# Columns of normalised x for two of four token chunks: DVE 32x32 block transposes and transfers within SBUF in the place of PE transpositions

## The chip, the cores and the metric

The kernel runs on one core of one Trainium2 chip. The metric is the device time of one execution in microseconds (us). Five engines work side by side, each with an instruction queue of its own that runs in order: PE (matmul), DVE (vector), ACT (scalar), POOL (GpSimd) and SP, whose queue here does little but issue DMA transfers.

## The reference

x is 2048 tokens of 576 numbers. Everything is float32.

```python
xn = _layernorm(x, axis=-1)                      # (x - mean) / sqrt(var + eps), per token
s  = _A_ref(xn, A_wqkv, A_wo)                    # attention, 32 heads of 18, then times wo
g  = _silu(_B_ref(xn, B_w_gate, B_w_up, B_w_down))   # ((xn Wg) * (xn Wu)) Wd, F = 4608
return x + s * g
```

Both branches multiply by xn from the left. PE sums over the partitions of its operands, so xn is wanted with its 576 columns on the partitions and the tokens along the free axis. This turning is what the change touches.

## The kernel before

**Precision.** Each float32 operand is split into a rounded high part and a low part (the rest); a product takes three terms. `xc`, the turned xn of a chunk, holds high parts in slots 0 to 3 (512 columns), low parts in slots 4 to 7, and the last 64 columns twice in slot 8 (high in partitions 0 to 63, low in 64 to 127).

**Stages.** A prologue of some 190 us makes q, k and v from xn; a main loop of some 2300 us does attention and the gated branch, two streams that share PE, in an order that a planner in the kernel has worked out and written down; a short end multiplies by wo. The change lies in the prologue, and the instructions from the main loop on stay as they are.

**The prologue** takes the tokens in four chunks of 512 (c = 0 to 3; a chunk is four tiles t of 128 tokens). Its order is the order of the code: each engine gets its instructions as the lines come.

- `load_x(c)` fetches a chunk to `xin` (two buffers). `norm(c)` makes its statistics and writes `xn` (one buffer), half a chunk at a time: chunk c+2 is normalised between blocks of chunk c.
- `to_columns(c)` turns `xn`: for each of five groups of 128 columns, four PE transpositions (128x128, with the identity) to a PSUM bank, an ACT copy for the high part, a DVE subtraction for the low part. So that the fifth group too has 128 columns, the last 64 columns are copied a second time into `xn[:, t, 576:640]` (line 374). `first_columns()` does the same for chunk 0.
- `qk_block(b, c)` makes 128 rows of q or k for a chunk: 14 matmuls to one PSUM bank (tags a and b in turn, two buffers each, so four in all), ACT copies the high part to `hl`, DVE subtracts for the low part, and SP stores `hl` to DRAM (`sqk`). `hl` has three buffers. I write c1b0 for block 0 of chunk 1.
- `v_block(t)` makes a tile of v with two banks of the four of tag g; ACT copies them to `vo` (three buffers before line 604), SP stores them (`sv`).
- `x_store(c, ks)` writes `xc` to DRAM for the gated branch, `w_fetch` and `v_fetch` load weights, `w_now` and `v_split` split them (ACT and POOL).

For c = 1 the order is: `load_x(3)`, c1b0 to c1b2, `to_columns(2)`, c1b3, `v_split(1)`, half of `norm(3)`, part of `x_store`, c1b4, the other half of `norm(3)`, part of `x_store`, c1b5, rest of `x_store`, `w_fetch(3)`, `v_block(0)` to `v_block(3)`, `w_fetch(4)`. For c = 2: c2b0 to c2b2, `to_columns(3)`, c2b3 to c2b5 with `x_store` of chunk 2. Then c3b0 follows.

**SP's queue** issues all these transfers in that order. The program gives them eight semaphores in turn, so each waits until the transfer eight places ahead of it has landed, besides what it waits for otherwise.

Of the kernel before, what the change touches and what calls it, by code (L numbers as in the profile page):

```python
# [41 lines left out]
def kernel(  # L42
# [10 lines left out]
    nc = tc.nc  # L53
    _, S, D = x.shape
# [5 lines left out]
    NCH = S // 512  # L60
# [8 lines left out]
    wpool = ctx.enter_context(tc.tile_pool(name="wpool", bufs=1))  # L69
    xcp = ctx.enter_context(tc.tile_pool(name="xcp", bufs=2))  # L70
# [25 lines left out]
    x2 = x.rearrange("o s d -> (o s) d")  # L96
# [3 lines left out]
    ep = early.enter_context(tc.tile_pool(name="early", bufs=1, side="right"))  # L100
# [123 lines left out]
    graw, gw, draw, dw = {}, {}, {}, {}  # L224
# [100 lines left out]
    xcs = [None] * NCH  # L325
    vstack, pro = ExitStack(), ExitStack()
    vp = vstack.enter_context(tc.tile_pool(name="vp", bufs=1))
    pp = pro.enter_context(tc.tile_pool(name="pro", bufs=1))
# [15 lines left out]
    xin, xns = {}, {}  # L344

    def load_x(c):
        xin[c] = ep.tile([128, 4, D], FT, name="xin", bufs=2)
        for t in range(4):
            nc.sync.dma_start(xin[c][:, t, :], x2[c * 512 + t * 128:c * 512 + t * 128 + 128, :])

# [2 lines left out]
    def norm_stats(c, t):  # L353
        st = ep.tile([128, 2, 6], FT, name="st", bufs=4)
        mv = ep.tile([128, 2], FT, name="mv", bufs=4)
        rs = ep.tile([128, 2], FT, name="rs", bufs=4)
        for g in range(2):
            nc.vector.bn_stats(st[:, g, :], xin[c][:, t, g * HALF:(g + 1) * HALF])  # L358
        nc.vector.bn_aggr(mv, st)
        nc.scalar.activation(rs[:, 0:1], mv[:, 1:2], AF.Sqrt, bias=eps)  # L360
        stat[c, t] = mv, rs

    def norm_apply(c, t):
        if t == 0:
            xns[c] = ep.tile([128, 4, 640], FT, name="xn", bufs=1)
        xn = xns[c]
        mv, rs = stat.pop((c, t))
        nc.vector.reciprocal(rs[:, 1:2], rs[:, 0:1])
        op = nc.vector.tensor_scalar(xn[:, t, 0:D], xin[c][:, t, :], mv[:, 0:1], rs[:, 1:2],  # L369
                                     op0=OP.subtract, op1=OP.mult)  # L370
        if c < 2 and t == 3:
            behind.append(op)
        if c:
            nc.vector.tensor_copy(xn[:, t, D:640], xn[:, t, 512:D])
        else:
            nc.scalar.activation(xn[:, t, D:640], xn[:, t, 512:D], AF.Copy)

    def norm(c, ts=range(4)):
        for t in ts:
            norm_stats(c, t)  # L380
        for t in ts:
            norm_apply(c, t)

    nqk = [0]

    def to_columns(c):

        xn = xns.pop(c)
        if c < 2:
            xc = pp.tile([128, 9, 512], FR, name="xcx", bufs=2)  # L390
        else:
            xc = xcp.tile([128, 9, 512], FR, name="xc")
        xcs[c] = xc
        for k in range(5):
            if k < 4:
                p = bank("g", 3)
            else:
                p = bank("a" if nqk[0] % 2 else "b", 2)
                nqk[0] += 1
            for t in range(4):  # L400
                nc.tensor.transpose(p[:, t * 128:(t + 1) * 128],
                                    xn[:, t, k * 128:(k + 1) * 128], ident)
            if k < 4:
                nc.scalar.activation(xc[:, k, :], p, AF.Copy)
                nc.vector.tensor_tensor(xc[:, 4 + k, :], p, xc[:, k, :].bitcast(FT),
                                        op=OP.subtract)
            else:
                nc.scalar.activation(xc[:, 8, :], p, AF.Copy)
                nc.vector.tensor_tensor(xc[64:128, 8, :], p[64:128, :],
                                        xc[64:128, 8, :].bitcast(FT), op=OP.subtract)  # L410
# [47 lines left out]
    def qk_block(b, c):  # L458
        w, ninth = (t[:, b % 2] for t in wq[b // 2])
        p = bank("a" if nqk[0] % 2 else "b", 2)  # L460
        nqk[0] += 1
        for n, (a, e) in enumerate(QK_PAIRS):
            nc.tensor.matmul(p, w[:, a, :] if a < 9 else ninth, xcs[c][:, e, :], start=n == 0,  # L463
                             stop=n == len(QK_PAIRS) - 1)
        hl = pp.tile([128, 2, 512], FR, name="hl", bufs=3)
        nc.scalar.activation(hl[:, 0, :], p, AF.Copy)
        nc.vector.tensor_tensor(hl[:, 1, :], p, hl[:, 0, :].bitcast(FT), op=OP.subtract)
        g0 = blocks[b]
        for kind in range(2):
            lo, hi = max(g0, kind * D), min(g0 + 128, (kind + 1) * D)  # L470
            if lo < hi:
                dst = sqk[kind, :, lo - kind * D:hi - kind * D, c * 512:(c + 1) * 512]
                nc.sync.dma_start(dst.rearrange("h r s -> r h s"), hl[lo - g0:hi - g0].bitcast(FT))
# [21 lines left out]
    def v_fetch(h):  # L495
        raw = vp.tile([128, 5, HALF], FT, name="wvraw", bufs=1)
        vbox["raw"] = raw
        c0 = 2 * D + h * HALF
        nc.sync.dma_start(raw[:, 0:4, :],
                          wqkv[0:512, c0:c0 + HALF].rearrange("(k p) c -> p k c", p=128))  # L500
        for b in (0, 64):
            nc.sync.dma_start(raw[b:b + 64, 4, :], wqkv[512:576, c0:c0 + HALF])
# [12 lines left out]
    def v_block(t):  # L515
        c, r = divmod(t, 4)
        ps = [bank("g", 3), bank("g", 3)]
        for h in range(2):
            for n, (a, e) in enumerate(PAIRS):
                nc.tensor.matmul(ps[h][:, 0:HALF], xcs[c][:, e, r * 128:(r + 1) * 128],  # L520
                                 vbox["w"][:, a, h * HALF:(h + 1) * HALF], start=n == 0,
                                 stop=n == len(PAIRS) - 1)
        v = vrows[vturn[0] % len(vrows)]
        vturn[0] += 1
        for h in range(2):
            nc.scalar.activation(v[:, 16 * h:16 * h + 16, 0:DH],
                                 ps[h][:, 0:HALF].rearrange("p (a b) -> p a b", b=DH), AF.Copy)
        nc.sync.dma_start(sv[t * 128:(t + 1) * 128], v)

    def w_now(i):  # L530
        wq[i], todo = w_split(raws[i], 1 if i == 4 else 2, ep if i == 2 else pp if i == 4 else None)
        for f, a in todo:
            f(*a)

    def w_fetch(i):
        raws[i] = w_load([(wqkv, b) for b in blocks[2 * i:2 * i + 2]])
# [30 lines left out]
    for c in range(NCH):  # L567
        if c + 2 < NCH:
            load_x(c + 2)
        for b in range(3):  # L570
            qk_block(b, c)
            if c == 0 and b == 0:
                w_now(2)
        if c + 1 < NCH:
            to_columns(c + 1)
        for b in range(3, 6):
            qk_block(b, c)
            if c == 1 and b == 3:
                v_split(c)
            if b < 5 and c + 2 < NCH:  # L580
                norm(c + 2, (0, 1) if b == 3 else (2, 3))
            if c in (1, 2):
                x_store(c, range(3 * (b - 3), 3 * (b - 2)))
            if c == 0 and b == 3:
                v_split(c)
            if c == 0 and b == 5:
                v_fetch(1)
            if c == NCH - 1 and b == 3:
                w_now(3)
        if c == 1:  # L590
            w_fetch(3)
            for t in range(4):
                v_block(t)
            w_fetch(4)
        if c == 2:
            w_now(4)
# [780 lines left out]
    with ExitStack() as end:  # L1377
        ep = end.enter_context(tc.tile_pool(name="end", bufs=1, reuse_waits="tile"))
# [44 lines left out]
        for i, t in enumerate(order):  # L1423
# [13 lines left out]
            y = ys[i % 4]  # L1437
# [3 lines left out]
            xt = xi.pop(t)  # L1441
# [40 lines left out]
```

## Time and profile before

| | |
|---|---|
| median of 3 runs | 2594.03 us (2592.9 to 2594.87) |
| profiled execution | 2593.44 us, span of its instructions 2591.3 us |
| busy: PE, DVE, ACT, POOL | 2582.0, 1813.5, 1550.6, 675.8 us |
| DMA | 435.65 MB in 186066 packets, mean 168 GB/s |
| granted PE clock | 1.0 |

The span counts from the first instruction; 2.1 us of the execution lie around it. In a row of the timeline stand the start, the length, engine, line, operation, output and inputs, the count of instructions merged into the row, and in brackets the idle time before the first of them and what ended it. A row of a line's instructions gives the shortest, median and longest duration in ns. For SP a duration is that of the issue, not of the transfer. A row of windows gives, for a stretch, busy time of each engine and at its end the granted PE clock, the mean busy share of the 16 DMA engines and the rate in GB/s.

### The profile page before, as it was taken

How to read it: one execution, taken by the hardware profiler on the slowest of the kernel's cores; microseconds unless marked ns; L12 is line 12 of the kernel's file. 1: busy time of each engine (PE TensorE's matmuls, PEld its weight loads, DVE VectorE, ACT ScalarE, POOL GpSimd, SP SyncE). 2: the span in 40 equal slices, each digit the busy share in tenths (PEclk: the TensorE clock that was granted, in tenths of full speed). 3: DMA queues.
4: the chain of work that ended last, by engine and by line, in shares of the span. 5: the costliest groups of instructions: out<-in, count | busy, mean ns of one | idle time of the engine just before them, and what ended most of it. 6: DMA issues, size and time to landing. Idle time of an engine off the chain costs nothing.

```text
span 2591.3 us, 59623 instructions
## 1 busy us (share of the span) xinstructions
PE 2582.0 (100%) x24440; PEld 2132.3 (82%) x24440; DVE 1813.5 (70%) x2996; ACT 1550.6 (60%) x3096; POOL 675.8 (26%) x697
## 2 busy tenths in 40 slices
PE   9999999999999999999999999999999999999999
PEld 7899877888888888888878887777887877877889
DVE  7209777777777778777777877777777777777238
ACT  4223677766766666666666666666666666666621
POOL 3114444434431222222111222111111222221016
PEclk9999999999999999999999999999999999999999
DMA  7899767677653444454444443444444444443357
GB/s 243 251 299 260 202 184 194 184 193 212 175 190 114 142 163 135 151 161 160 142 168 149 142 140 127 138 145 159 121 158 124 145 150 141 133 140 112 124 204 252
DMA packets 186066, 435.65 MB, mean 168 GB/s; under 512 B 51041, under 2 KB 111105, under 8 KB 155585
## 3 DMA queue, kind: packets, MB, share of 16 engines
q1 hardware_dynamic: 183632, 423.88, 53.0%
q0 software_dynamic: 2160, 7.96, 0.8%
q8 instruction: 192, 3.15, 0.5%
q14 instruction: 82, 0.66, 0.1%
HBM read 315.16 MB, written 111.35 MB: 165 GB/s over the span
## 4 chain that ended last, share of the span: by engine, by line
PE 97%; DVE 1%; DMA 1%; ACT 0%; issue 0%; SPq 0%; ACTq 0%; DVEq 0%
PE pg L775 36%; PE pg L734 17%; PE pg L836 16%; PE pa L671 11%; PE pb L723 9%; PE pg L520 2%; PE pb L463 2%; PE pa L463 1%; PE pg L1431 1%; DMA sqk<-hl 1%; PE pb L1431 1%; PE pa L1431 1%; DVE st L358 0%; DMA wgu<-swg 0%; DVE xn L369 0%; PE pa L723 0%
## 5 line engine op out<-in xcount | busy, mean ns | idle before, releaser
L673 DVE TENSOR_REDUCE mx<-pa 128x1 f32<-128x512 f32 x2016 | 1348.8, 687 | 331.9 <-PE pa L671 156.3
L775 PE MATMUL pg<-xc,wgu 64*128 64x512 f32 x7776 | 1442.5, 392 | 0.4 <-DMA wgu<-swg 0.3
L725 ACT ACTIVATE pt<-pb 128x512 f32<-128x512 f32 x2005 | 1144.5, 602 | 471.3 <-PE pb L723 369.0
L775 PEld LDWEIGHTS pg<-xc,wgu 64*128 64x128 f32 x7776 | 1078.8, 186 | 45.5 <-issue 0.8
L836 PE MATMUL pg<-wd,hs 64*128 64x288 f32 x6816 | 877.7, 293 | 0.0
L836 PEld LDWEIGHTS pg<-wd,hs 64*128 64x128 f32 x6816 | 815.2, 185 | 11.6 <-issue 0.8
L671 PE MATMUL pa<-whole,turning 54*128 54x512 f32 x1999 | 783.2, 399 | 0.3 <-DVE mx L673 0.3
L723 PE MATMUL pb<-whole,turning 56*128 56x512 f32 x1978 | 775.2, 398 | 0.0
L734 PE MATMUL pg<-pt,vt 128*32 128x512 f32 x4096 | 453.3, 594 | 0.1
L671 PEld LDWEIGHTS pa<-whole,turning 54*128 54x128 f32 x1999 | 363.3, 184 | 75.3 <-issue 53.0
L816 POOL TENSOR_TENSOR hs<-us,hs 128x512 fp32r<-128x512 f32 x144 | 186.0, 1292 | 866.4 <-ACT hs L800 610.0
L863 POOL TENSOR_TENSOR acc<-acc,st 128x288 f32<-128x288 f32 x284 | 229.5, 810 | 606.0 <-ACT st L893 341.0
L723 PEld LDWEIGHTS pb<-whole,turning 56*128 56x128 f32 x1978 | 360.0, 184 | 5.7 <-ACT pt L725 0.2
L734 PEld LDWEIGHTS pg<-pt,vt 128*32 128x32 f32 x4096 | 126.2, 110 | 285.1 <-issue 279.2
L740 DVE TENSOR_TENSOR oc<-oc,pg 128x512 f32<-128x512 f32 x35 | 24.1, 688 | 221.2 <-PE pg L734 214.9
L257 POOL TENSOR_TENSOR wgu<-wraw,wgu 128x384 fp32r<-128x384 f32 x108 | 108.1, 1014 | 215.3 <-ACT wgu L256 97.6
L738 ACT ACTIVATE oc<-pg 128x512 f32<-128x512 f32 x32 | 19.1, 598 | 229.4 <-PE pg L734 222.0
L899 DVE TENSOR_TENSOR acc<-acc,pg 128x288 f32<-128x288 f32 x261 | 116.3, 448 | 38.5 <-PE pg L836 34.5
L792 DVE TENSOR_TENSOR us<-pg,us 128x512 f32<-128x512 f32 x144 | 98.6, 685 | 54.0 <-PE pg L775 50.9
L893 ACT ACTIVATE st<-pg 128x288 f32<-128x288 f32 x284 | 117.1, 413 | 27.0 <-PE pg L836 19.9
L785 ACT ACTIVATE us<-pg 128x512 f32<-128x512 f32 x143 | 85.5, 598 | 76.6 <-PE pg L775 65.4
L800 ACT ACTIVATE hs<-us 128x512 fp32r<-128x512 f32 x142 | 89.4, 630 | 15.9 <-DVE us L792 15.4
(154 smaller groups left out, 1288.8 us busy)
## 6 DMA issues: line engine op xcount, KB each, us to landing
wgu<-swg SPq DMA_DIRECT2D x102, 1152.0 KB
wd<-swd SPq DMA_DIRECT2D x50, 1152.0 KB
swg<-wgu SPq DMA_DIRECT2D x36, 1152.0 KB
whole<-sqk SPq DMA_DIRECT2D x192, 144.0 KB
turning<-sqk SPq DMA_DIRECT2D x384, 72.0 KB
swd<-wd SPq DMA_DIRECT2D x18, 1152.0 KB
sqk<-hl SPq DMA_DIRECT2D x32, 512.0 KB
xc<-sx SPq DMA_DIRECT2D x24, 512.0 KB
```

The source lines that it names most:

```text
L257: nc.gpsimd.tensor_tensor(w[:, 9 + b:12 + b, :], raw[:, b:b + 3, :], w[:, b:b + 3, :].bitcast(FT), op=OP.subtract)
L671: nc.tensor.matmul(p, q[rows, t * 128:(t + 1) * 128], k[rows, c * 512:(c + 1) * 512], start=True, stop=True)
L673: nc.vector.tensor_reduce(mx[h][:, t, c:c + 1], p, axis=AX.X, op=OP.max)
L723: nc.tensor.matmul(p, k[rows, t * 128:(t + 1) * 128], q[rows, c * 512:(c + 1) * 512], start=True, stop=True)
L725: nc.scalar.activation(pt[t, c // 2][:, c % 2, :], p, AF.Exp, scale=scale)
L734: nc.tensor.matmul(p[32 * c:32 * c + 32, :], vt[h // 2][:, t, 6 * (h % 2):6 * (h % 2) + 32], pt[t, c // 2][:, c % 2, :], start=t == ts[0], ...
L775: nc.tensor.matmul(ps, gw[n][half[r], a, :], xg[i][half[r], e, :], start=k == 0, stop=k == len(TERMS) - 1)
L816: nc.gpsimd.tensor_tensor(hj[:, 1, :], h32, hj[:, 0, :].bitcast(FT), op=OP.subtract)
L836: op = nc.tensor.matmul(ps[:, 0:HALF], hs[u][half[r], j, a, s * 128:(s + 1) * 128], dw[u][half[r], j, e, i * HALF:(i + 1) * HALF], start=( ...
L863: nc.gpsimd.tensor_tensor(a, a, st, op=OP.add)
L893: nc.scalar.activation(st, ps[:, 0:HALF], AF.Copy)
L899: nc.vector.tensor_tensor(a, a, ps[:, 0:HALF], op=OP.add)
```

## The change

Chunks 2 and 3 no longer go through PE.

- `load_x` fetches these chunks with another spread: partition 32a+j gets tokens 128a + 32t + j for t = 0 to 3; four transfers of 32 partitions x 4 rows, in the place of four of 128 partitions x 1 row, with the same bytes and rows.
- The copy of the last 64 columns (line 374) goes for these chunks, eight copies in all.
- `turn_blocks(c)`, after the second half of `norm(c)`, does four DVE transposes (128x576, every 32x32 block turned in place), from `xn` into the space of `xin`.
- `move_blocks(c, parts)` brings the turned blocks to their partitions: 32 transfers within SBUF for a chunk, issued by SP, 16 of 32 partitions x 4 x 512 B (64 KB, to `xt`) and 16 of 32 partitions x 512 B (16 KB, to `xr`; two copies of the last 64 columns). For chunk 2 all 32 stand where `to_columns(2)` stood; for chunk 3 eight follow the store of each of the first four `v_block`s.
- `late_columns(c)` makes the high parts (ACT) and low parts (DVE) as `to_columns` did, from SBUF and not from PSUM: for chunk 2 after `v_block(1)`, for chunk 3 where `to_columns(3)` stood.
- `xt` and `xr` use space that is free at that time (tags `wd`, `draw`, and a buffer of `xin`).

```diff
     def load_x(c):
         xin[c] = ep.tile([128, 4, D], FT, name="xin", bufs=2)
+        if c > 1:
+            for a in range(4):
+                r0 = c * 512 + a * 128
+                nc.sync.dma_start(xin[c][32 * a:32 * a + 32], x2[r0:r0 + 128, :].rearrange("(t j) d -> j t d", j=32))
+            return
...
-        if c:
+        if c == 1:
             nc.vector.tensor_copy(xn[:, t, D:640], xn[:, t, 512:D])
-        else:
+        elif c == 0:
...
+    def turn_blocks(c):
+        xn = xns.pop(c)
+        y = xin.pop(c).rearrange("p t d -> p (t d)").rearrange("p (b t j) -> p b t j", b=18, t=4)
+        for t in range(4):
+            nc.vector.transpose(y[:, :, t, :], xn[:, t, 0:D].rearrange("p (b j) -> p b j", j=32))
+        xraw.setdefault(c, [None, None, None])[0] = y
...
+    def move_blocks(c, parts):
+        y = xraw[c][0]
...
+        main, rest = xraw[c][1:]
+        for a in parts:
+            src = y[32 * a:32 * a + 32].rearrange("p b t j -> p b (t j)")
+            for b in range(4):
+                nc.sync.dma_start(main[32 * b:32 * b + 32, :, a, :],
+                                  src[:, 0:16, :].rearrange("p (k b) q -> p k b q", b=4)[:, :, b, :])
+                nc.sync.dma_start(rest[32 * b:32 * b + 32, a, :], src[:, 16 + b % 2, :])
...
+    def late_columns(c):
+        main, rest = xraw.pop(c)[1:]
+        xc = xcs[c] = xcp.tile([128, 9, 512], FR, name="xc")
+        for k in range(4):
+            x = main[:, k].rearrange("p a q -> p (a q)")
+            nc.scalar.activation(xc[:, k, :], x, AF.Copy)
+            nc.vector.tensor_tensor(xc[:, 4 + k, :], x, xc[:, k, :].bitcast(FT), op=OP.subtract)
+        x = rest.rearrange("p a q -> p (a q)")
+        nc.scalar.activation(xc[:, 8, :], x, AF.Copy)
+        nc.vector.tensor_tensor(xc[64:128, 8, :], x[64:128], xc[64:128, 8, :].bitcast(FT), op=OP.subtract)
...
-        if c + 1 < NCH:
-            to_columns(c + 1)
+        if c == 0:
+            to_columns(1)
+        elif c == 1:
+            move_blocks(2, range(4))
+        elif c == 2:
+            late_columns(3)
         for b in range(3, 6):
             qk_block(b, c)
...
             if b < 5 and c + 2 < NCH:
                 norm(c + 2, (0, 1) if b == 3 else (2, 3))
+                if b == 4:
+                    turn_blocks(c + 2)
...
             for t in range(4):
                 v_block(t)
+                move_blocks(3, (t,))
+                if t == 1:
+                    late_columns(2)
             w_fetch(4)
```

Three places in the order of the instructions matter below. The first is DVE's queue while chunk 0 is worked on: the end of `norm(2)`, and behind it the low parts of blocks c0b5 (`pb`) and c1b0 (`pa`). Before:

```order
L368 RECIPROCAL rs<-rs 128x1
L369 TENSOR_SCALAR xn<-xin,mv,rs 128x576
L374 COPY xn<-xn 128x64
L467 TENSOR_TENSOR hl<-pb,hl 128x512
L467 TENSOR_TENSOR hl<-pa,hl 128x512
```

and with the change:

```order
L373 RECIPROCAL rs<-rs 128x1
L374 TENSOR_SCALAR xn<-xin,mv,rs 128x576
L397 STREAM_TRANSPOSE xin<-xn 128x18x32 x4
L507 TENSOR_TENSOR hl<-pb,hl 128x512
L507 TENSOR_TENSOR hl<-pa,hl 128x512
```

The four transposes stand ahead of the low part of c0b5, for whose end its store waits. The second place is SP's queue from the store of c1b0 on, with the semaphores that each transfer waits for (`DMAHW` 0 to 7 are the eight of the transfers). Before:

```order
L473 DMA sqk<-hl 128x2x512 [waits DMAHW7_49,DVE_49]
L473 DMA sqk<-hl 64x2x512 [waits DMAHW0_49,DVE_49]
L473 DMA sqk<-hl 64x2x512 [waits DMAHW1_49]
L473 DMA sqk<-hl 128x2x512 [waits DMAHW2_49,DVE_49]
L473 DMA sqk<-hl 128x2x512 [waits DMAHW3_49,DVE_49]
L542 DMA sx<-xcx 128x512 [waits DMAHW4_49]
```

and with the change:

```order
L513 DMA sqk<-hl 128x2x512 [waits DMAHW7_49,DVE_49]
L513 DMA sqk<-hl 64x2x512 [waits DMAHW0_49,DVE_49]
L513 DMA sqk<-hl 64x2x512 [waits DMAHW1_49]
L513 DMA sqk<-hl 128x2x512 [waits DMAHW2_49,DVE_49]
L413 DMA xt<-xin 32x4x128 [waits DMAHW3_49]
L415 DMA xr<-xin 32x128 [waits DMAHW4_49]
L413 DMA xt<-xin 32x4x128 [waits DMAHW5_49]
L415 DMA xr<-xin 32x128 [waits DMAHW6_49]
L413 DMA xt<-xin 32x4x128 [waits DMAHW7_49]
```

The moves of chunk 2 go on for 32 transfers, and the store of c1b3, which followed that of c1b2, comes behind them; the fifth move waits for the semaphore that the store of c1b0 raises. The third place is ACT's queue at c1b5 and the first tiles of v. Before:

```order
L360 ACTIVATE rs<-mv,eps 128x1 x2
L466 ACTIVATE hl<-pa 128x512
L526 ACTIVATE vo_438<-pg 128x16x18 x2
L526 ACTIVATE vo_440<-pg 128x16x18 x2
L526 ACTIVATE vo_442<-pg 128x16x18 x2
```

and with the change:

```order
L365 ACTIVATE rs<-mv,eps 128x1 x2
L506 ACTIVATE hl<-pb 128x512
L566 ACTIVATE vo_436<-pg 128x16x18 x2
L566 ACTIVATE vo_438<-pg 128x16x18 x2
L423 ACTIVATE xc<-xt 128x512 x4
L426 ACTIVATE xc<-xr 128x512
L566 ACTIVATE vo_440<-pg 128x16x18 x2
```

The high parts of chunk 2 stand between the copies of the second and the third tile of v, and wait there for the moves. The five of chunk 3 come likewise behind the copy of c2b2.

More of the change, by code (lines that the diff above doesn't have):

```diff
@@ L384 @@
     nqk = [0]
+    xraw = {}
+    def turn_blocks(c):
[6 more added lines that the diff above has]
+        y = xraw[c][0]
+        if c == 2:
+            box = wpool.tile([128, 2, 4, 128], FT, name="xr", tag="draw", bufs=1)
+            xraw[2][1:] = wpool.tile([128, 4, 4, 128], FT, name="xt", tag="wd", bufs=1), box[:, 0]
+            xraw.setdefault(3, [None, None, None])[2] = box[:, 1]
+        elif xraw[c][1] is None:
+            xraw[c][1] = ep.tile([128, 4, 4, 128], FT, name="xt3", tag="xin", bufs=2)
+        main, rest = xraw[c][1:]
[15 more added lines that the diff above has]
+        nc.vector.tensor_tensor(xc[64:128, 8, :], x[64:128], xc[64:128, 8, :].bitcast(FT), op=OP.subtract)
     def to_columns(c):
         xn = xns.pop(c)
[L389 to L392, printed above, removed]
+        xc = pp.tile([128, 9, 512], FR, name="xcx", bufs=2)
         xcs[c] = xc
```

## The prediction

> **What bounds the kernel now.** I read the page first, for the engine that bounds.
>
> ```profile
> PE 2582.0 (100%) x24440; PEld 2132.3 (82%) x24440; DVE 1813.5 (70%) x2996; ACT 1550.6 (60%) x3096; POOL 675.8 (26%) x697
> PE 97%; DVE 1%; DMA 1%; ACT 0%; issue 0%; SPq 0%; ACTq 0%; DVEq 0%
> ```
>
> PE is busy for 2582.0 of 2591.3 us, and 97% of the chain that ended last is PE. So a PE instruction that goes is time won, and anything that keeps PE waiting is time lost; nothing later takes it back, since there is no idle time of PE to take it from. The question is who makes PE wait in the prologue once the transpositions are gone. The timeline of PE around them:
>
> ```profile
> 42.95 1.91 PE L401 MATMUL pg<-identr,xn 128*128 128x128 f32 x16
> 44.70 0.60 PE L401 MATMUL pb<-identr,xn 128*128 128x128 f32 x4
> 45.05 3.22 PE L463 MATMUL pa<-xcx,wgu 128*128 128x512 f32 x13
> ...
> 62.80 7.70 PE L520 MATMUL pg<-wv,xcx 128*128 128x288 f32 x56 [0.36 <-ACT vo L526]
> 70.34 3.13 PE L463 MATMUL pb<-xc,wgu 128*128 128x512 f32 x13
> ...
> 79.89 1.91 PE L401 MATMUL pg<-identr,xn 128*128 128x128 f32 x16
> 81.63 0.60 PE L401 MATMUL pa<-identr,xn 128*128 128x128 f32 x4
> 81.99 3.22 PE L463 MATMUL pb<-xc,wgu 128*128 128x512 f32 x13
> ...
> 91.79 3.13 PE L463 MATMUL pa<-xc,wgu 128*128 128x512 f32 x13
> ```
>
> Twenty transpositions hold PE from 42.95 to 45.05 and from 79.89 to 81.99. At 62.80, `v_block(2)`, stands the one wait of this stretch, 0.36 us for ACT: here PE already runs level with the engines behind it. 70.34 is c2b0, the first reader of chunk 2's columns, 91.79 is c3b0, the first of chunk 3's. Who holds ACT back is in ACT's and SP's timelines (SP's row is the issue; several are merged):
>
> ```profile
> 45.29 0.60 ACT L466 ACTIVATE hl<-pa 128x512 fp32r<-128x512 f32 x1 [4.67 <-PE pb L401]
> 45.78 2.07 ACT L404 ACTIVATE xc<-pg 128x512 fp32r<-128x512 f32 x4
> 53.06 0.60 ACT L466 ACTIVATE hl<-pa 128x512 fp32r<-128x512 f32 x1 [4.72 <-DMA sqk<-hl]
> ...
> 61.87 0.58 ACT L466 ACTIVATE hl<-pa 128x512 fp32r<-128x512 f32 x1
> 62.35 1.30 ACT L526 ACTIVATE vo<-pg 128x288 f32<-128x288 f32 x4
> ```
>
> ```profile
> 39.92 0.36 SPq L473 DMA_DIRECT2D sqk<-hl  x1
> 40.38 0.42 SPq L499 DMA_DIRECT2D wvraw<-in_A_wqkv_dram  x1
> ...
> 45.25 9.53 SPq L473 DMA_DIRECT2D sqk<-hl  x5
> ...
> 64.05 0.37 SPq L473 DMA_DIRECT2D sqk<-hl  x1
> ...
> 72.13 3.82 SPq L528 DMA_DIRECT2D sv<-vo  x4
> ```
>
> The store of c0b5 is issued at 39.92. At 45.25 SP goes on with the store of c1b0, at 45.29 ACT with c1b2; both wait for the semaphore of c0b5's store, so that it landed then, and the releaser PE in the row is only the latest that the profile knows. The store of c1b0 frees its `hl` buffer at 53.06, which starts c1b3's copy; from there ACT and DVE work in a chain (two statistics halves between) to 61.87 and to the copy of v at 62.35, for which PE waits. So a stretch of PE's time hangs on when c0b5's store is issued.
>
> **The change part by part.**
>
> 1. PE loses 2 x 2.10 = 4.2 us.
>
> 2. DVE gets four transposes ahead of c0b5's low part:
>
> ```profile
> 38.19 0.20 DVE L374 COPY xn<-xn 128x64 f32<-128x64 f32 x1
> 38.30 0.16 DVE L368 RECIPROCAL rs<-rs 128x1 f32<-128x1 f32 x1
> ...
> 39.21 0.68 DVE L467 TENSOR_TENSOR hl<-pb,hl 128x512 fp32r<-128x512 f32 x1
> ...
> 46.53 2.47 DVE L405 TENSOR_TENSOR xc<-pg,xc 128x512 fp32r<-128x512 f32 x4
> ```
>
> ```profile
> L747 DVE STREAM_TRANSPOSE od<-oc x32: 697/702/711, 348.5 to 2481.6; 128x512 f32<-128x512 f32 x32
> ```
>
> A 128x512 transpose takes 702 ns, so 576 columns 0.79; back to back such operations overlap (four subtractions of 0.68 in 2.47), so 0.70 each, 2.8 us. Two copies that go there save 0.11 each (the next instruction starts 0.11 after it). c0b5's low part moves from 39.21 to 41.8, 2.6 us, and its store, on which the weights, the load of chunk 3 and the store of c1b0 queue behind, with it: c1b0 lands at 53.06 + 2.6 = 55.7. In the chain from there two more copies go, one of them in a slow stretch (0.7 us in all); the transposes of chunk 3 come behind all that ACT needs. So ACT's copy of v is at 62.35 + 2.6 - 0.7 = 64.3 and `v_block(2)` starts at 64.7, where PE, 2.1 us early and without its old wait of 0.36, would be at 60.35: a wait of 4.3, and PE is 1.9 later than before. c2b0 could start at 72.2.
>
> 3. SP issues 64 more transfers, between stores it issued before. No row has 32 partitions. The nearest:
>
> ```profile
> L754 SPq DMA_DIRECT2D sot<-oc x128: 264/314/610, 351.7 to 2485.2; - x128
> L349 SPq DMA_DIRECT2D xin<-in_A_x_dram x16: 328/430/584, 0.7 to 44.1; - x16
> L555 SPq DMA_DIRECT2D xc<-xcx x36: 461/596/1439, 157.1 to 191.5; - x36
> ```
>
> L754 has 18 partitions, L349 128, L555 64 and is the only one within SBUF. An issue lies between 0.31 and 0.60; I take 0.48, near L555's shortest, since its median falls in a stretch of full DMA engines and the moves do not. What they transfer is no bound: per pair 160 packets of 512 B, and this stretch carried such packets almost alone:
>
> ```profile
> q1 hardware_dynamic: 848, 0.43, 64.9%
> ```
>
> (17 to 20 us: packets, MB, share of 16 engines), 0.649 x 3 x 16 / 848 = 37 ns each, 0.37 us a pair, against two issues of 0.96. Both chunks together are 12 us of DMA time.
>
> 4. When chunk 2 lands. The first four moves go out early; the fifth waits for c1b0's store (55.7), the ninth for the first four, which queue behind the stores of c1b1 and c1b2, at about 58.5. 24 x 0.48 end at 70.0. Landing takes some 2 us:
>
> ```profile
> 0.74 1.82 SPq L349 DMA_DIRECT2D xin<-in_A_x_dram  x4
> 3.55 0.82 DVE L358 BATCH_NORM_STATS2 st<-xin 128x6 f32<-128x288 f32 x2 [2.06 <-DMA xin<-in_A_x_dram]
> ```
>
> (2.8 from the start of the first issue to its reader, with 288 KB that need 0.9 at 330 GB/s.) So 72.0, the first high part 0.6 later, and c2b0 starts at 72.6, not 72.2; it then follows ACT's pace of 0.5 a slot (row 45.78) where PE takes 0.24 (13 matmuls in 3.13), 0.8 more. PE is 3.1 us behind the time before.
>
> 5. When chunk 3 lands. From 70.0 SP has what it had between the store of c1b3 and the stores of v: three stores, twelve `x_store` transfers and six of weights, 4.8 MB. Before, part of this ran beside PE's blocks; now all of it stands behind the moves. At the rates of a full stretch,
>
> ```profile
> core 0: us, PE busy (x) PEld busy (x) DVE busy (x) ACT busy (x) POOL busy (x), PEclk, DMA share, GB/s
> 44.00:47.00 3.00, 3.00 (x21) 2.66 (x20) 1.08 (x2) 1.71 (x4) 0.00 (x0) 1.00 1.09 269
> 47.00:50.00 3.00, 3.00 (x15) 2.45 (x14) 2.70 (x5) 1.34 (x3) 0.00 (x0) 1.00 1.05 395
> 50.00:53.00 3.00, 3.00 (x15) 2.42 (x14) 0.00 (x0) 0.00 (x0) 0.00 (x0) 1.00 1.06 342
> ```
>
> 4.8 MB / 368 GB/s = 13 us: 83.0 for the first store of v (72.13 before). Then four times a store (0.4) and eight moves (3.84): 100.0, landed 102.0, c3b0 at 102.6 and 0.8 more in its block. Before it stood at 91.79: 11.6 us late. PE, having done c2b0 to c2b5 by 93, waits some 9 of them. ACT waits for the same moves with c2b3 to c2b5 behind it, whose four banks just hold PE's blocks, so nothing is added there. After it the two sides keep step: stores trail by a few us and the four banks and three `hl` buffers cover that. Nothing later moves.
>
> Other edits cost nothing while their cover lasts: ACT and DVE do the same ten operations from SBUF as from PSUM. The loads of x keep their bytes and row length, so 0 for them. The Trainium skill has a rule against that (SBUF — State Buffer, "Door 1: The DMA port swizzle": bandwidth follows how many of 16 ports the partitions reach, and 32 reach half of them). By the rule and its 435 GB/s the load of chunk 3 (1.18 MB) would go at 218 GB/s, 5.4 us against 4.4 at the 269 of the row from 44 to 47, an estimate; the sum would be 1 us more. No row here shows a load to 32 partitions.
>
> Sum, against the profiled execution's 2593.44 (0.6 under the median 2594.03): 2593.44 + 11.6 = **2605.0 us**. In 11.6 the 4.2 of step 1 are already taken off.
>
> **The rivals.**
>
> A, not slower: the issue is cheap. Some 56 issues lie in a row on the way to c3b0, so 0.05 of their price is 2.8 us. At L754's 0.314 the sum is 2605.0 - 56 x 0.166 = 2595.7, within 0.2% of before; below 0.37 (2598.8) it is no longer slower by 0.2%. Then c3b0 hardly waits, and what remains is the delay of step 2. For it: 264 ns occur. Against: L555, the nearest in kind, never goes below 0.461. The Trainium skill leans this way (DMA: Bandwidth & Descriptors, "Issuing engines are not separate DMA queues": the sequencer's time to start a DMA is usually small beside the DMA itself); by it the pair would go at its 0.37 of data and the time would be A's. Row L555 speaks against the rule.
>
> B, the gain is kept: c1b0 lands at 53.06 because the DMA engines are full (share 1.05 from 47 to 53), not because of SP's order, and the moves fit in. Then 2593.44 - 4.2 = 2589.2. Against it: the batch ahead of c1b0 begins with c0b5's store, and moves with it.
>
> C, the moves cost more than their issue: 32 partitions are slow, or each eight wait for a landing of over 4 us. At L555's median 0.596 the sum is 2605.0 + 56 x 0.116 = 2611.5, and more if landing grows.
>
> **How the numbers follow.** Forecast (issue 0.42 to 0.56, 2601 to 2610): 0.52. A: 0.25. C: 0.16. B: 0.07. From A's 2595 to C's 2612 the range leaves out B and the far part of C, under 2 in 10. A measurement here tells 0.2%, 5.2 us, from no change: under 2588.8 falls the lower part of B, 0.04; within, A and the rest of B, 0.28; above, 0.68.
>
> **What would show it.** Right: no L401 rows at 42.95 and 79.89 but those of chunk 1; c0b5's store issued near 42.5; PE waiting at `v_block(2)` for some 4 us and at c3b0 for some 9, the releaser ACT (L423) and behind it the moves; SP's rows for the moves without gaps at about 0.48. Wrong: moves issued at 0.3, or SP waiting between them; c0b5's store still near 40; c3b0 without a wait, which would leave about 2596; a wait after 115 us, which I have priced at nothing.

## The result, and the profile after

| | before | after |
|---|---|---|
| median on one chip | 2593.47 us (2592.73 to 2594.87, 4 runs) | 2624.97 us (2623.26 to 2627.11, 4 runs) |
| profiled execution, its span | 2593.44, 2591.3 us | 2623.26, 2621.5 us |

The ratio is 1.0121, 95% interval 1.0108 to 1.0134: 31.5 us slower. The forecast was 2605.0, its range ended at 2612. The direction was right, the size was not.

The page of after, the same two rows as before:

```profile
PE 2587.7 (99%) x24400; PEld 2128.0 (81%) x24400; DVE 1815.9 (69%) x2996; ACT 1551.1 (59%) x3096; POOL 676.1 (26%) x697
PE 94%; SPq 2%; DMA 1%; DVE 1%; issue 1%; ACT 0%; POOL 0%; ACTq 0%; DVEq 0%; POOLq 0%
```

Two things stand here. SPq, the issue on SP's queue, is now 2% of the chain that ended last. And PE is busy for 5.7 us more with 40 instructions less. Span less busy time is 33.8 us, before 9.3, so 24.5 us of the 30.2 by which the span grew are idle PE. The other 5.7 are matmuls that took longer: 9.9 us more, less the 4.2 of the transpositions that went. The timeline of PE gives the places:

```profile
59.26 3.76 PE L560 MATMUL pg<-wv,xcx 128*128 128x288 f32 x13 [3.85 <-ACT wv L551]
63.38 11.61 PE L560 MATMUL pg<-wv,xcx 128*128 128x288 f32 x85 [0.35 <-POOL wv L552]
78.98 5.56 PE L503 MATMUL pa<-xc,wgu 128*128 128x512 f32 x13 [3.99 <-ACT xc L423]
97.84 4.58 PE L503 MATMUL pa<-xc,wq 128*128 128x512 f32 x13 [3.55 <-DVE hl L507]
118.22 6.20 PE L503 MATMUL pa<-xc,wgu 128*128 128x512 f32 x13 [12.30 <-ACT xc L423]
...
124.64 3.12 PE L503 MATMUL pb<-xc,wgu 128*128 128x512 f32 x13
```

The waits sum to 24.0 us. c3b0 (118.22) stood at 91.79 before, c3b1 (124.64) at 94.99. PE is 29.65 us late there, and no later wait of note comes; the loss is made in the first 125 us. The first column of the windows' rows below is the stretch, the third number from the end the granted PE clock: 0.69 and 0.50 behind the waits at 78.98 and 118.22, 1.00 soon after.

```profile
78.98:84.50 5.52, 5.47 (x14) 0.69 1.03 349
118.22:124.30 6.08, 6.08 (x14) 0.50 0.93 295
127.82:130.90 3.08, 3.08 (x15) 1.00 1.03 380
```

Now SP's queue. Its rows, and the two rows that group the moves (shortest, median, longest issue in ns):

```profile
53.71 0.69 SPq L413 DMA_DIRECT2D xt<-xin  x1
...
61.33 0.63 SPq L413 DMA_DIRECT2D xt<-xin  x1
62.01 0.58 SPq L415 DMA_DIRECT2D xr<-xin  x1
62.64 0.63 SPq L413 DMA_DIRECT2D xt<-xin  x1
...
76.89 0.60 SPq L415 DMA_DIRECT2D xr<-xin  x1
92.93 0.53 SPq L568 DMA_DIRECT2D sv<-vo  x1
93.50 0.69 SPq L413 DMA_DIRECT2D xt<-xin  x1
...
115.92 0.60 SPq L415 DMA_DIRECT2D xr<-xin  x1
```

```profile
L413 SPq DMA_DIRECT2D xt<-xin x32: 626/632/694, 53.7 to 115.2; - x32
L415 SPq DMA_DIRECT2D xr<-xin x32: 537/597/635, 54.8 to 115.9; - x32
```

From 61.33 to 62.64 a pair takes 1.31 us, 0.655 a move with the gaps, where the forecast took 0.48. From there on the issues lie end to end, as it said; the first eight, from 53.71 to 61.33, lie further apart. Meanwhile the DMA engines are nearly idle: share 0.31 and 0.43 in the two stretches of moves, 0.93 between them, where all that had waited goes out.

```profile
61.00:77.50 16.50, 13.64 (x94) 13.04 (x92) 9.56 (x22) 3.05 (x9) 2.32 (x3) 0.93 0.31 60
77.50:93.50 16.00, 14.47 (x54) 11.15 (x55) 3.19 (x5) 3.30 (x7) 0.00 (x0) 0.89 0.93 299
93.50:116.50 23.00, 8.88 (x32) 6.51 (x30) 1.89 (x3) 2.18 (x5) 0.00 (x0) 0.81 0.43 115
```

DVE's and ACT's rows say who waits for that:

```profile
40.15 2.76 DVE L397 STREAM_TRANSPOSE xin<-xn 128x576 f32<-128x576 f32 x4
42.83 0.65 DVE L507 TENSOR_TENSOR hl<-pb,hl 128x512 fp32r<-128x512 f32 x1
```

```profile
58.28 0.60 ACT L506 ACTIVATE hl<-pb 128x512 fp32r<-128x512 f32 x1 [9.01 <-DMA sqk<-hl]
...
95.86 0.71 ACT L566 ACTIVATE vo<-pg 128x288 f32<-128x288 f32 x2 [14.26 <-DMA sv<-vo]
...
117.54 2.19 ACT L423 ACTIVATE xc<-xt 128x512 fp32r<-128x512 f32 x4 [19.49 <-DMA xr<-xin]
119.63 0.62 ACT L426 ACTIVATE xc<-xr 128x512 fp32r<-128x512 f32 x1
122.17 0.60 ACT L506 ACTIVATE hl<-pb 128x512 fp32r<-128x512 f32 x1 [1.92 <-DMA sqk<-hl]
124.37 0.60 ACT L506 ACTIVATE hl<-pa 128x512 fp32r<-128x512 f32 x1 [1.60 <-DMA sqk<-hl]
```

The four transposes take 2.76 us ahead of c0b5's low part. c1b0's store lands at 58.28, before 53.06. The first store of v, at 92.93 where it was at 72.13, holds ACT's copies until 95.86; the last move of chunk 3 holds them from 98 to 117.54; then the late stores of q and k do.

### The profile page after: what moved, and what is told of

Its sections match the earlier page's. It is cut to its first block, busy times and chain, and to the rows that moved or that the text cites. A ratio compares the mean times of both kernels' runs of the same rounds, so it can differ in the third digit from the quotient of the medians.

```text
span 2621.5 us, 59633 instructions
## 1 busy us (share of the span) xinstructions
PE 2587.7 (99%) x24400; PEld 2128.0 (81%) x24400; DVE 1815.9 (69%) x2996; ACT 1551.1 (59%) x3096; POOL 676.1 (26%) x697
## 4 chain that ended last, share of the span: by engine, by line
PE 94%; SPq 2%; DMA 1%; DVE 1%; issue 1%; ACT 0%; POOL 0%; ACTq 0%; DVEq 0%; POOLq 0%
PE pg L824 36%; PE pg L783 17%; PE pg L885 16%; PE pa L720 11%; PE pb L772 9%; PE pg L560 2%; PE pg L1480 1%; DMA sqk<-hl 1%; PE pb L503 1%; PE pa L503 1%; SPq L413 1%; SPq L415 1%; PE pb L1480 1%; PE pa L1480 1%; DMA wvraw<-in_A_wqkv_dram 0%
```

## The experiments

The theories: **S**, what costs is the time for which the moves' issue holds SP's queue, with the stores of hl and v behind it. Its rivals are **D**, the moves' bytes on the DMA engines; **V**, DVE's transposes ahead of c0b5's store; **W**, the late columns on ACT and DVE; **X**, the loads of x to 32 partitions; **K**, the lower clock behind a wait. Medians of before beside them lay at 2593.2 to 2594.1.

### 1. The price of an issue by itself

Ahead of the kernel before and its own transfers, eight transfers of each of several shapes (four of those to DRAM). SP's stand alone up to 22 us; the groups of ACT's queue (from 22.7 us) and of POOL's (from 30.7) ran beside SP's later ones:

```
+ for i in range(8):                            # the shape of a main move
+     nc.sync.dma_start(bdst[32*(i%4):32*(i%4)+32, 4*(i//4):4*(i//4)+4, 0:128], v4[0:32, :, 0:128])
+ ...                                           # 128 partitions; to and from DRAM; from ACT, POOL
```

> The kernel before, with ten groups of four or eight transfers of unused data ahead of everything else (this adds time at the start, of no interest; the look is at the duration of the issues). SP: 32 partitions x 4 x 512 B within SBUF to another quadrant, 32 x 512 B within SBUF, 32 x 2 KB within one quadrant, 128 x 512 B within SBUF, 64 x 512 B within SBUF, 32 x 4 x 512 B from SBUF to DRAM, 128 x 512 B to DRAM, 32 x 4 x 512 B from DRAM, 16 x 512 B within SBUF; then the first form from ACT's queue and from POOL's. Theory S (the price of 0.63 and 0.60 us lies in the issue itself, by form): the first two forms cost 0.60 to 0.65 here too, where nothing else runs, 16 KB as much as 64 KB, and a DRAM side or 128 partitions bring it to 0.3 to 0.45. Rival D (back pressure from full DMA engines): the first forms cost 0.3 to 0.45 here, and bytes decide. For POOL's queue I expect 0.6 to 1.0, for ACT's as on SP.

The rows are, in order: 32 partitions x 4 x 512 B within SBUF, 128 x 512 B within SBUF, 128 x 512 B to DRAM, 32 x 4 x 512 B from DRAM, and 32 x 4 x 512 B within SBUF from POOL's queue.

```profile
L80 SPq DMA_DIRECT2D bdst<-bsrc x8: 594/601/754, 3.3 to 8.0; - x8
L86 SPq DMA_DIRECT2D bdst<-bsrc x8: 591/599/601, 18.8 to 23.3; - x8
L92 SPq DMA_DIRECT2D bdr<-bsrc x4: 430/459/595, 31.9 to 33.5; - x4
L94 SPq DMA_DIRECT2D bdst<-in_A_x_dram x8: 430/436/470, 34.0 to 37.4; - x8
L100 POOL DMA_DIRECT2D bdst<-bsrc x8: 548/548/689, 30.7 to 34.7; - x8
```

With nothing beside it a transfer within SBUF costs SP 0.60 us, as much with 128 partitions as with 32; for 128 I had expected 0.3 to 0.45. Other shapes there, 8 KB to 64 KB, took 0.587 to 0.596. The 128-partition store to DRAM and the load from DRAM went at 0.44 to 0.46, but a 32-partition store to DRAM took 0.60 too. I had read L555's 0.596 as the effect of full DMA engines; it is the plain price.

### 2. The same moves, read by nobody

PE's transpositions stay, DVE transposes nothing, x is loaded as before; the 64 moves are issued from whatever stands in the buffer.

```
- to_columns(c + 1)
+ to_columns(2); move_blocks(2, range(4))       # c == 1; moves of chunk 3 behind each v_block
```

> PE transpositions for all chunks as before, no DVE transposes, loads of x as before; the 64 moves are issued at the same places of SP's queue as in the change, of x as it was loaded, and nothing reads what they bring. Theory S (SP's queue is held up by 64 issues of 0.66 and everything behind them is late): copies of v and of blocks c2b0 on wait for stores that are issued 15 to 35 us later than before, the copy of c2b3 for the store of c2b0 (issued near 113), PE finds no free bank at c3b1 near 98 and waits to 116: 2608 to 2614 us. Rival W (only the wait for the moved data costs): 2593 to 2597. Rival D (DMA engines overloaded): under 2600, with no long waits of SP's making.

2619.44 us (2619.11 to 2624.44), ratio 1.0106 (1.0091 to 1.0121): +26 us, more than I expected of S. Nothing of V, X and W is in this kernel. PE waits in two other places:

```profile
91.36 1.97 PE L441 MATMUL pg<-identr,xn 128*128 128x128 f32 x8 [11.28 <-ACT vo L566]
119.26 5.51 PE L503 MATMUL pb<-xc,wgu 128*128 128x512 f32 x13 [10.85 <-DVE hl L507]
```

One is a bank that waits for ACT's copy of v, whose buffer waits for SP's store; the other waits for an `hl` buffer in the same way. So the late queue reaches PE through the stores as well as through the columns.

### 3 and 4. One chunk alone

Chunk 2 alone, and chunk 3 alone, is turned by DVE; PE turns the other.

```
- if c > 1:      # quarters of x
+ if c == 2:     # (run 4: c == 3); to_columns() for the other chunk, its moves left out
```

> Chunk 2 by DVE and transfers, chunk 3 by PE as before. Theory S: the moves of chunk 2 end at 77.5 and c2b0 starts at 79 as in the change; without the 32 of chunk 3 the stores of c2 are issued some 21 us earlier, c3b0 starts near 103 (91.8 before, 118.2 in the change): 2602 to 2607 us. Rival W, with each chunk's wait priced alone: c2b0's 8.6 late and its slow block: also 2602 to 2605. Rival V (DVE's transposes ahead of the low part of c0b5 are the cause): nearly the whole 31 us, 2618 or more, since they are all here.

> Chunk 2 by PE as before, chunk 3 by DVE and transfers. Theory S: the first store of v at 72 as before, then four times a store and eight moves of 0.66, ending at 96; c3b0 starts near 98 (one set of transpositions less would let it start at 89.7) and its block is slow by 3: 2600 to 2605 us. Together with the other half this is well under the 31 us of both, since the second 32 moves no longer stand behind the first. Rival V: no loss ahead of c0b5, so under 2596.

Chunk 2 alone 2609.14 us (1.0062, 1.0047 to 1.0077), chunk 3 alone 2606.15 (1.0049, 1.0033 to 1.0066). Both lie just above what S gave; chunk 2 alone, which has V's transposes, does not reach V's 2618. Their sum, 16 + 13 us, is nearly all of the 31.5, so that the two losses add up; I had expected the two together well under it. With chunk 2 alone PE loses most at to_columns(3), for the store of v; with chunk 3 alone at c3b0:

```profile
94.71 1.97 PE L444 MATMUL pg<-identr,xn 128*128 128x128 f32 x8 [4.15 <-ACT vo L569]
```

```profile
102.08 5.59 PE L507 MATMUL pb<-xc,wgu 128*128 128x512 f32 x13 [9.92 <-ACT xc L424]
```

### 5. The transposes later

```
-         if b == 4:
-             turn_blocks(c + 2)
+     if b == 5 and c + 2 < NCH:                # behind block 5's low part
+         turn_blocks(c + 2)
```

> The changed kernel with the four transpositions of a chunk issued on DVE after block 5's low part, no longer ahead of it, so that block 5's store leaves about 2.8 us earlier. Theory S (SP's queue, by the length of the moves' issue, decides): the moves start a little earlier but take as long, 2620 to 2624 us, and chunk 3's first block still starts near 116 us. Theory V (the late store of chunk 0's block 5 is what grows into the loss): below 2612 us.

2621.72 us (2621.24 to 2622.81), ratio 1.011 (1.0095 to 1.0125). V is small, some 3 us, and its interval overlaps that of the changed kernel; the trace agrees, as c1b0's store lands at 55.52 here and at 58.28 there. c3b0 still starts at 115.93.

### 6. The loads of x alone

```
+ if c > 1:                                      # in the kernel before, nothing else changed
+     for a in range(4):
+         nc.sync.dma_start(xin[c][32*a:32*a+32], ...rearrange("(t j) d -> j t d", j=32))
+     return
```

> The kernel before with one edit alone: x of chunks 2 and 3 is loaded in quarters, 32 partitions to a transfer (the tokens of these chunks then stand in another order, so that the output differs). Theory X (transfers to 32 partitions take longer and hold up the stores that share the machine with them): chunk 1's first block lands 1 to 2 us later than at 53.06, and the time is 2594 to 2597 us. If such loads cost nothing, as the forecast had it: 2592 to 2594.5 us, with block 3's buffer in chunk 0 free at 29.2 us as before.

2597.48 us (2595.41 to 2599.22), ratio 1.0014 (1.0005 to 1.0024). The forecast had these loads at 0; the interval says 1.3 to 6.2 us. The windows from 24 to 30 us, while chunk 2's x is loaded, first before, then with quarters:

```profile
24.00:30.00 6.00, 6.00 (x28) 4.88 (x27) 2.40 (x5) 1.34 (x3) 2.13 (x5) 1.00 1.00 341
```

```profile
24.00:30.00 6.00, 6.00 (x31) 4.98 (x30) 3.03 (x5) 1.48 (x4) 2.93 (x5) 1.00 1.03 258
```

All 16 engines are busy in both, at 341 and at 258 GB/s (282 in the changed kernel in that stretch). The first `hl` buffer that waits behind this came free at 29.19 before, at 31.58 here. ACT's copy of c1b3, which c1b0's store frees, started at 53.06 before and at 56.96 here (the row names PE as its releaser, whose matmuls for that copy were done by 55.6), and c2b0 at 70.34 and at 74.19. X holds, by more than the 1 to 2 us I gave that store. The Trainium skill's rule that the forecast weighed and left at 1 us (SBUF — State Buffer, "Door 1: The DMA port swizzle") goes in this direction; by it the rate would halve, by the rows it fell by a quarter, with other transfers in the same stretch.

### 7. Chunk 3 alone, its moves on POOL's queue

```
- nc.sync.dma_start(main[...], ...); nc.sync.dma_start(rest[...], ...)      # from run 4
+ nc.gpsimd.dma_start(main[...], ...); nc.gpsimd.dma_start(rest[...], ...)
```

> Only chunk 3 turned by DVE, as in the earlier run of 2606.2 us, but its 32 moves are issued on POOL's queue, where nothing else is issued from 58 to 110 us. At 0.55 to 0.60 us apiece they end near 88 us, ahead of chunk 3's first block at 91.8. Theory S (what costs is the time for which other transfers stand behind the moves on SP's queue): the loss goes, 2590 to 2595 us. If it is the moves' data, the transposes or the late columns on ACT and DVE that cost: 2603 us or more, as with SP's queue.

2595.38 us (2594.64 to 2596.73), ratio 1.0007 (0.9997 to 1.0017), against 2606.15 with SP's queue. The same moves, bytes, transposes and late columns cost 11 us less on a queue on which nothing else waits. It is 0.4 us above the range given, and does not show PE's 2.1 us.

### 8. No idle PE ahead of c3b0

```
+ warm_g(50)        # 50 matmuls of no use, after the last of chunk 2's blocks and ahead of c3b0
```

> The changed kernel with 50 matmuls of no use put on PE between the last block of chunk 2 that it can do and chunk 3's first block, about 11 us of work that fills most of the wait of 12.3 us there. Theory K (the granted clock of 0.50 in the 6.2 us behind that wait is a cost of its own, about 3 us): chunk 3's first block runs at a granted clock near 1 in 3.1 to 3.6 us and the time is 2620.5 to 2623 us. If the clock costs nothing, or falls anyway: 2624 to 2627 us.

2624.17 us (2623.8 to 2624.75): no gain, theory K falls as a cost of its own.

```profile
118.42 4.14 PE L509 MATMUL pa<-xc,wgu 128*128 128x512 f32 x13
122.39 0.39 PE L509 MATMUL pa<-xc,ninth 128*128 128x512 f32 x1
125.01 3.24 PE L509 MATMUL pb<-xc,wgu 128*128 128x512 f32 x13 [2.23 <-DVE hl L513]
```

The block takes 4.14 us in place of 6.20, at a granted clock of 1.00 from 118 to 124 us, and then c3b1 waits for an `hl` buffer and starts at 125.01; in the changed kernel it starts at 124.64 without that wait. Two limits stood at the same moment, and taking one away shows the other: the stores behind the moves.

### 9, 10, 11. Through DRAM, with 10 issues for a chunk

The transposes stand late as in run 5. Each chunk's blocks go to DRAM and come back as columns:

```
+ nc.gpsimd.dma_start(turned[c-2, :, :, a, :].rearrange("b i q -> i b q"), y[32*a:32*a+32]...)     # 4
+ nc.gpsimd.dma_start(main[:, k]..., turned[c-2, 4*k:4*k+4].rearrange("b i a q -> (b i) (a q)"))   # 4, and 2 for rest
  # runs 9 and 11: x in one transfer for 128 partitions, from four runs of 32 rows
+ xs = x2[c*512:c*512+512, :].rearrange("(a t j) d -> t a j d", t=4, j=32)
+ for t in range(4): nc.sync.dma_start(xin[c][:, t, :], xs[t])
```

> A version meant to keep the gain: DVE transposes after block 5's low part; a chunk's blocks then go on POOL's queue to a buffer in DRAM in 4 transfers and come back as columns in 6 (10 issues for a chunk in place of 32, none of them on SP's queue), and x of chunks 2 and 3 is loaded in the same token order by transfers that each fill 128 partitions. 4.7 MB are moved in place of 2.4 MB. Theory S (SP's queue) with X (loads to 32 partitions are slow): both losses go, PE's 4.2 us are kept in part or whole, 2589 to 2592.5 us. If the data or the work of DVE and ACT on the late columns cost: 2595 us or more.

> As the run before, but with x of chunks 2 and 3 loaded in quarters, 32 partitions to a transfer, as in the changed kernel. Theory X: 1.5 to 4 us more than the run before, as the quarters alone made the kernel before 3.7 us slower. If the shape of these loads costs nothing here: within 1 us of it.

> As the first of these runs, but its 10 transfers for a chunk are issued on SP's queue, where the loads also wait there for the stores' landing. Theory S: some 5 to 6 us of issue and 2 to 4 us of waiting for each chunk stand ahead of the stores of hl and vo, 2594 to 2603 us. If only the number of issues over 50 matters and the queue takes up 20 more: 2589 to 2592.5 us.

Run 9: 2614.08 us (1.0078, 1.0065 to 1.0092). Run 10: 2599.16 (1.0021, 1.0013 to 1.003). Run 11: 2626.03 (1.0127, 1.0111 to 1.0142). These are misses: the "wide" loads of x made run 9 some 15 us slower than the quarters of run 10. PE's wait in run 9, and the window of its load of x:

```profile
76.26 3.69 PE L564 MATMUL pg<-wv,xcx 128*128 128x288 f32 x13 [17.11 <-ACT wv L555]
```

```profile
24.00:30.00 6.00, 6.00 (x28) 4.87 (x27) 1.98 (x4) 0.47 (x1) 1.92 (x4) 1.00 0.61 200
```

The DMA engines are busy for 0.61 where it was 1.00, at 200 GB/s, while stores wait behind the loads. So the load is slow and leaves engines idle. The Trainium skill has a rule that would give this (DMA: Bandwidth & Descriptors, "Why a DMA increments its semaphore by 16 and not by 1"): a transfer is spread over as many engines as divide the outermost size of both of its sides. Here that is 4, of the four runs of rows, against 128. The share agrees with few engines; that it was four, no row here shows. Run 11 has these loads too, so it tells of SP's queue only by its 12 us over run 9. In run 10 PE loses 3.81 us at the v weights, as c1b0's store lands at 57.46. Run 5, with the same loads and the same late transposes, has 2.03 us and 55.52. The 1.9 us between them go to the transfers to DRAM beside that store, as far as two traces tell: with SP's queue free, the bytes do cost something in that full stretch.

### 12. All moves on POOL's queue

```
- nc.sync.dma_start(...)                          # both moves of move_blocks()
+ nc.gpsimd.dma_start(...)
```

> The changed kernel with all 64 moves issued on POOL's queue and nothing else changed. At 0.53 us apiece chunk 2's end near 61 us and hold up POOL's low parts of the v weights by 2 to 4 us; chunk 3's end near 88. Theory S: most of the loss goes, 2594 to 2601 us. If the moves cost by their data or the late columns: 2615 us or more.

2610.05 us (2609.26 to 2610.48), ratio 1.0063 (1.005 to 1.0077): half of the loss goes, not most. What is left is new:

```profile
62.69 2.80 PE L560 MATMUL pg<-wv,xcx 128*128 128x288 f32 x9 [6.34 <-ACT wv L551]
69.42 16.03 PE L560 MATMUL pg<-wv,xcx 128*128 128x288 f32 x89 [3.93 <-POOL wv L552]
```

POOL's low parts of the v weights stand behind chunk 2's moves, which run from 44 to 68 us on POOL. They start earlier than on SP and run beside c1b0's store, which lands at 61.70 and not at 58.28. This left D open, and led to the next two.

### 13 and 14. Issues without bytes, bytes without issues

Both are run 2 with the unread moves reshaped: 64 moves of 4 KB, and the bytes of all 64, in packets of 512 B, in 16 (these stay within their 32 partitions).

```
+ nc.sync.dma_start(main[32*b:32*b+32, 0, a, 0:32], src[:, b, 0:32])       # 13: and one more to rest
+ nc.sync.dma_start(main[32*a:32*a+32]..., src16[:, 0:16])                 # 14: one for all b,
+ nc.sync.dma_start(rest[32*a:32*a+32], src16[:, 0:4])                     #     one for rest
```

> The kernel before, PE's transpositions kept, with 64 transfers on SP's queue where the changed kernel has its moves, as in the run of 2619.4 us, but each moves only 128 B in 32 partitions (4 KB), 0.26 MB in all in place of 2.4 MB; nothing reads them. Theory S (time of issue on SP's queue): 0.55 to 0.60 us apiece as before, 2615 to 2620 us. Theory D (the bytes of the moves, which share the machine with the stores of hl and vo): 2594 to 2600 us.

> As the run before, but the 2.4 MB of the changed kernel's moves, in the same packets of 512 B, go in 16 transfers in place of 64 (for each 32 partitions one of 256 KB and one of 64 KB); nothing reads them. Theory S: about 10 us of issue in place of 40, 2594 to 2601 us. Theory D: 2615 us or more, as with 64.

Run 13: 2619.01 us, ratio 1.0094 (1.008 to 1.0108). Run 14: 2594.18, ratio 1.0003 (0.9994 to 1.0012). The issues in run 13, its window from 61 to 72 us, and the first store of v; then that window and that store in run 14:

```profile
L410 SPq DMA_DIRECT2D xt<-xin x32: 507/588/976, 49.1 to 109.6; - x32
```

```profile
61.00:72.00 11.00, 10.52 (x76) 10.04 (x75) 3.14 (x10) 3.10 (x9) 0.00 (x0) 1.00 0.06 8
```

```profile
87.93 0.53 SPq L567 DMA_DIRECT2D sv<-vo  x1
```

```profile
61.00:72.00 11.00, 10.54 (x74) 9.99 (x73) 2.76 (x9) 2.81 (x8) 0.00 (x0) 1.00 1.00 360
74.10 0.53 SPq L567 DMA_DIRECT2D sv<-vo  x1
```

With a ninth of the bytes the DMA engines stand at a share of 0.06 and the loss is whole; with all of the bytes and a quarter of the issues (medians 0.80 and 0.66 us) there is none. S is shown, and D falls as the cause of this loss; that bytes delay a store beside them, as in runs 10 and 12, is another cost. The Trainium skill names this bound (Perfetto Trace Analysis, "What 'DMA-bound' means": an issuing engine's track solid with DMA slices, whose time is the making of descriptors). Its advice for it, large descriptors, is not what helped here: the packets were 512 B in run 14 too, and fewer transfers did it.

### 15 and 16. The found costs taken away

x is loaded as before; ACT and DVE put the tokens in order as they read the columns. Run 15 is run 5 with that, run 16 is run 7 with that.

```
- x = main[:, k].rearrange("p a q -> p (a q)")
+ x = main[:, k].rearrange("p a (t j) -> p t a j", j=32)      # written through "p (t a j) -> p t a j"
```

> The changed kernel with the transpositions after block 5's low part, and with x of chunks 2 and 3 loaded as in the kernel before; ACT and DVE put the tokens back in order when they split the columns, by the order in which they read. Theory X (the loads to 32 partitions cost 2 to 3.7 us): 2618 to 2620 us, against 2621.7 with the loads in quarters. Theory S alone: 2621 to 2623 us, since chunk 3's first block waits for the moves in either case.

> Only chunk 3 turned by DVE, its moves on POOL's queue (2595.4 us with the loads in quarters), now with x loaded as in the kernel before and the tokens put back in order as in the run before this. All the costs found are taken away and PE is spared 2.1 us: 2590.5 to 2593.5 us. If the moves' 1.2 MB or the late columns cost by themselves: 2594 us or more.

Run 15: 2619.06 us, ratio 1.0095 (1.0079 to 1.011), 2.7 us under run 5. That leaves +25, as in run 13 (+25) and near run 2 (+26). ACT's copy of c1b3, which c1b0's store frees, shows V and X apart: it starts at 58.28 with both, at 55.52 in run 5 (X alone) and at 52.82 here (neither; 52.08 to 53.36 in the kernel before and in runs 2, 13 and 14). So V, X and S make up the loss. The reading in another order costs nothing that shows: ACT's four copies took 2.19 us in either order. Run 15 also has 4.2 us less of PE than runs 2 and 13, and the late columns (W), which those lack. Neither shows, as PE waits for SP's queue in all three; whether W would cost something without that wait, run 15 does not tell.

Run 16: 2594.8, ratio 1.0004 (0.9995 to 1.0013), no different from before; the 2.1 us of PE do not show. In its profiled execution c3b0 starts at 90.09, 1.70 earlier than before; then

```profile
88.88 2.20 ACT L423 ACTIVATE xc<-xt 128x512 fp32r<-128x512 f32 x4 [6.49 <-DMA xt<-xin]
...
101.98 0.60 ACT L509 ACTIVATE hl<-pa 128x512 fp32r<-128x512 f32 x1 [4.17 <-DMA sqk<-hl]
...
110.27 1.54 ACT L129 ACTIVATE wgu<-wraw 128x512 fp32r<-128x512 f32 x4
```

```profile
110.94 1.20 PE L506 MATMUL pb<-xc,wgu 128*128 128x512 f32 x4 [0.98 <-ACT wgu L129]
```

ACT waits for the landed columns with hl's copies behind that wait, the stores of hl come in a bunch, and ACT's high part of the next weights is at 110.27 in place of 105.20. PE waits for them, and the block after stands at 114.77, before 114.23. The gain is turned into a wait for the weights. This chain is read from one trace, and no run takes it away. Nothing tried beat the kernel before.

## Why the prediction was wrong, point by point

1. **PE loses 4.2 us.** Right: 40 instructions fewer. As the forecast said, this does not count where PE waits for the columns.
2. **The transposes ahead of c0b5's store.** 2.76 us measured, 2.8 forecast. But c0b5's store went out at 43.52, not near 42.5, and c1b0's landed at 58.28, not 55.7. The rest is theory X, priced at 0: with X and without V it landed at 55.52, with neither at 52.82. The wait of 3.85 us came a little earlier than at `v_block(2)`, at the v weights, whose high parts stand on ACT behind the same landing.
3. **The price of an issue, the step that failed.** 0.48 was taken, 0.655 measured (0.60 to 0.63 and a gap). The nearer price stood in the row L555, median 0.596; I argued it away by the full engines, and run 1 shows it with nothing beside it. Of 56 moves that is 56 x 0.175 = 9.8 us, the largest part of the 18 us by which PE is later at c3b1 than forecast (29.65 against 11.6). The data were no bound, as forecast (share 0.31 beside the moves).
4. and 5. **The sum up to c3b0**, forecast 102.6, measured 118.22:

| term | forecast | measured | more |
|---|---|---|---|
| ninth move starts | 58.5 | 61.33 | 2.8 |
| to the last move of chunk 2 | 11.5 | 16.2 | 4.7 |
| to the first store of v | 13.0 | 15.4 | 2.4 |
| stores of v and moves of chunk 3 | 17.0 | 23.6 | 6.6 |
| landing to c3b0 | 2.6 | 1.7 | -0.9 |

   Together 15.6. The stretch between went at 299 GB/s, not 368. Then "After it the two sides keep step" failed: the block of c3b0 took 6.20 us and not 3.9, and run 8 shows that without the lower clock the stores would have held c3b1 to the same time. That adds 2.4 and makes 29.65 of the span's 30.2.

The mechanism forecast, SP's queue, is the one the runs show; but it was followed along one path, the columns. Run 2 shows that the late stores of v and of q and k alone cost 26 us, so that landing the columns sooner would not have saved the kernel. The forecast had put that path at nothing ("Nothing later moves"), trusting four banks and three `hl` buffers to cover it. Rival C, with a chance of 0.16, was nearest; at 0.655 its sum would have been 2614.8, still 8.5 short of the profiled 2623.26. Rival A falls with run 1, B with the late landing of c1b0's store and all that followed. The Trainium skill's rule cited for A (issue usually small beside the DMA) does not hold for these moves: 1.31 us of issue for a pair, against 0.37 of data by the forecast's estimate.

## What to carry to other kernels

Before a step is moved to many small transfers, count the issues on the queue they join, price each at the row nearest in kind (median, not minimum) with the gap, and list what stands behind them: here 64 x 0.655 = 42 us on SP ahead of stores whose buffers PE needs. A queue can be the bound while the DMA engines stand at a share of 0.06 to 0.4, so look at the issue rows and the share side by side; fewer transfers help, and another queue only as far as nothing waits on it. And where a wait is taken away and the time stays, look for the second limit that stood behind it.

## What the runs showed of the hardware

- SP took 0.59 to 0.60 us to issue a transfer within SBUF, whether 8 KB or 64 KB (run 1), 0.59 for 4 KB (run 13) and 0.60 to 0.63 in the changed kernel; POOL took 0.55, ACT 0.61 (run 1, beside SP's transfers).
- Loads to 32 partitions at a time ran with all engines busy and 258 GB/s in place of 341 (run 6; 282 in the changed kernel); a load of 128 partitions from four runs of rows left the engines busy for 0.61 (run 9).
- PE's granted clock was 0.50 for 6.1 us behind a wait of 12.3 us and 0.69 over 5.5 us behind one of 4.0. The Trainium skill (TensorE: Matmul & The Clock Gate, "Part 1: The HAM clock gate (the 'warmup' mystery)") has half clock until some 3.4 us of sustained work; the direction agrees, the stretch at 0.50 was longer here, where PE followed ACT's pace.
